# Storing the last column part of the last tile pair as two tiles on two queues

## Chip, cores, metric

One core of one Trainium2 chip. The metric is device time in microseconds (us), from repeated executions. The time before was 287.44 us, the median of 3 runs (287.15 to 287.49).

The span of a profile runs from the first to the last instruction of one execution; it is about 1.2 us shorter than the device time of that execution (286.2 and 287.46 us for the kernel before). I call "tail" the time from the end of the last evacuation out of PSUM to the end of the span. That is the part that the change can touch.

## The reference, cut to what matters

```python
# x is [1, 2048, 640], all bf16
g = sigmoid((x * gate_w).sum(-1, keepdims=True))
a = linear_attention(x, wqkv, w_phi) @ wo        # 32 heads of 20
b = (gelu(x @ w_gate) * (x @ w_up)) @ w_down     # hidden size 1728
return g * a + (1 - g) * b                       # [1, 2048, 640]
```

Only the final projections and the store of the output matter here. The kernel accumulates `@ wo` and `@ w_down` of a tile pair (2 x 128 rows) in PSUM, scales by a gate while it evacuates to SBUF, and stores.

## The kernel before

The work is laid out by hand, with explicit semaphores. A helper `sc.dma(queue, ...)` makes the issuing engine wait for everything the transfer reads, then issues; `sc.finish` makes SyncE wait for every engine and every DMA at the end. The last tile pair is done in three column parts (256, 256 and 128 columns), so that the first parts are stored while TensorE works on the next:

```python
def evac(h):                                   # column part h of the pair
    w0, w = sum(widths[:h]), widths[h]
    for j in (0, 1):                           # the two tiles of the pair
        bk, dst, g = banks[h][j], self.outsb[:, os_ + j, w0:w0 + w], self.Gm[:, ts[j]:ts[j] + 1]
        rd, wr = [("ps", bk), "Gm"], [("outsb", os_ + j, h)]
        if last and j == 1:
            sc.op("dve", lambda e: e.tensor_scalar(dst, self.bank(bk, w), g, None, op0=ALU.mult), reads=rd, writes=wr)
        else:
            sc.op("act", lambda e: e.activation(dst, self.bank(bk, w), AF.Copy, scale=g), reads=rd, writes=wr)
    if last:
        hs, c0, c1 = [h], w0, w0 + w
    # ... (other pairs: one store of all 640 columns; 'rows' is the output's view of the pair)
    sc.dma("sp", lambda e: e.dma_start(rows[:, :, c0:c1], self.outsb[:, os_:os_ + 2, c0:c1]),
           reads=[("outsb", os_ + j, k) for j in (0, 1) for k in hs], writes=[("out", t0, h)])
```

So tile 0 is evacuated by ScalarE and tile 1 by VectorE, and one store on SyncE's queue waits for both. The experiments also touch the warm-up, which keeps TensorE busy until the first load lands:

```python
for n in (512, 512, 512, 512, 512, 512, 128):
    sc.op("pe", lambda e: e.matmul(self.bank(0, n), ones[:, 0:P], ones[:, 0:n], start=True, stop=True),
          writes=[("ps", 0)])
```

The softmax here doesn't subtract the row's maximum and nothing guards it: scores larger than these inputs give would overflow.

Of the kernel before, what the change touches and what calls it, by code (L numbers as in the profile page):

```python
# [107 lines left out]
class _Kernel:  # L108
# [596 lines left out]
    def down_pair(self, t0, banks, widths):  # L705

        sc = self.sc
        ts = (t0, t0 + 1)
        NFC, KD = self.NFC - 1, self.KD
        nw = len(widths)  # L710
        hk = t0 // 4
        last = t0 + 2 == self.NT
        os_ = t0 % 4

        def mm(r, j, h, c, opens, x, n):
            t = ts[j]
            tt, gs, bk, w0, a = t % 4, t % 8, banks[h][j], sum(widths[:h]), 64 * r
            w, end = widths[h], x == n - 1
            if c <= NFC:
                lhs, rhs = self.hT(hk, c)[a:a + 64, tt * P:(tt + 1) * P], self.wd_sb[a:a + 64, c, w0:w0 + w]  # L720
                rd = [("hT", hk, c), "wd"] if c < NFC else [("hT", hk, 13, r), ("wd13", r)]
            else:
                k = c - NFC - 1
                lhs, rhs = self.goT[a:a + 64, gs, k, :], self.wo_sb[a:a + 64, k, w0:w0 + w]
                rd = [("goT", gs), "wo"]
            sc.op("pe", lambda e: e.matmul(self.bank(bk, w), lhs, rhs, start=opens and x == 0, stop=end and not opens,  # L726
                                           skip_group_check=True),
                  reads=rd, writes=[("ps", bk)] + ([("turn", bk)] if end else []), signal=end,
                  after=[("turn", bk)] if x == 0 and not opens else ())

        def evac(h):
            w0, w = sum(widths[:h]), widths[h]
            for j in (0, 1):
# [8 lines that stand above are left out]
            elif h == nw - 1:  # L742
                hs, c0, c1 = range(nw), 0, self.D
            else:
                return
            if t0 < self.TB:
                rows = self.out[0:self.BT, :].rearrange("(p j) n -> p j n", j=self.TB)[:, t0:t0 + 2, :]
            else:
                rows = self.out[t0 * P:(t0 + 2) * P, :].rearrange("(j p) n -> p j n", p=P)
            sc.dma("sp", lambda e: e.dma_start(rows[:, :, c0:c1], self.outsb[:, os_:os_ + 2, c0:c1]),  # L750
                   reads=[("outsb", os_ + j, k) for j in (0, 1) for k in hs], writes=[("out", t0, h)])

        wos = [NFC + 1 + k for k in range(KD)]
        opening = list(range(NFC + 1)) + wos
        for part in (range(NFC + 1), range(NFC + 1, len(opening))):
            for h in range(nw):
                for x in part:
                    for r in (0, 1):
                        mm(r, r, h, opening[x], True, x, len(opening))
                    yield None  # L760
        closing = list(range(NFC)) + wos
        for h in range(nw):
            for x, c in enumerate(closing):
                for r in (0, 1):
                    mm(r, 1 - r, h, c, False, x, len(closing))
                if c == closing[-1]:
                    evac(h)
                yield None
# [95 lines left out]
```

## Time and profile before

| What | Value |
|---|---|
| span | 286.2 us |
| TensorE busy | 281.8 us, 98% |
| last matmul starts | 283.49 us |
| last evacuation ends | 284.14 us |
| tail | 2.08 us |

The page of the kernel before, parts 1 and 4: busy time of each engine, and the chain of waits that ended last. TensorE is nearly the whole of both.

```profile
PE 281.8 (98%) x3017; PEld 186.7 (65%) x3032; DVE 174.9 (61%) x353; ACT 104.5 (37%) x199; POOL 5.3 (2%) x36
...
PE 98%; issue 0%; ACT 0%
```

The timeline of its end. Columns: start in us, length in us, engine, line, operation, tiles. SPq is SyncE's queue and ACTq ScalarE's; their length is that of the issue (the issuing engine's part in setting a transfer off), not of the transfer.

```profile
283.74 0.35 DVE L737 TENSOR_SCALAR outsb<-ps,Gm 128x128 bf16<-128x128 f32 x1 [0.52 <-PE ps L726]
283.77 0.37 ACT L739 ACTIVATE outsb<-ps,Gm 128x128 bf16<-128x128 f32 x1 [0.53 <-PE ps L726]
284.17 0.73 SPq L750 DMA_DIRECT2D out_dram<-outsb  x1
```

The issue begins right after both evacuations, and it is long: the stores of the first and of the second part took 0.370 and 0.372 us to issue, this one 0.735. It is not a wait for the data. The Trainium skill, "Perfetto Trace Analysis", section "Per-instruction lifecycle: what the profiler-reported window actually captures", says that the reported window of such a DMA opens when all its semaphores are satisfied, and that the movement of the data lies outside it. The trace agrees on both: the window opens at 284.17 with the evacuations done at 284.14, and the packets leave later, at 285.42. What fills the extra 0.36 us is then something behind the semaphores.

The DMA queues in the window from 283.5 to 284.6 us of the kernel before show one transfer on the instruction queue (q8); columns: packets, MB, share of 16 engines. The trace's single DMA records place it: one record of 16 KB at 283.56 to 284.52. I call it the fetch. It seems to sit on one DMA engine, as only one of the 16 completions of the store before came late (285.67, the others by 285.11).

```profile
q8 instruction: 1, 0.02, 5.4%
```

### The profile page before, as it was taken

The numbers are of one execution on the slowest core, as the hardware profiler recorded it, in microseconds if no ns is written. First come the engines' busy times: TensorE is split into PE (matmuls) and PEld (weight loads), VectorE is DVE, ScalarE is ACT, GpSimd is POOL, SyncE is SP. The second block draws the span as 40 slices with busy tenths as digits, with TensorE's granted clock in tenths as the row PEclk, the third lists the DMA queues.
The fourth block names the chain that finished last, engine by engine and source line by source line (L and its number), as shares of the span: only waits on it lengthen the run. The fifth ranks groups of instructions, "written<-read, shape, count | busy, mean of one in ns | idle before, by whom it ended". The sixth has DMA issues, their size and how long they took to land.

```text
span 286.2 us, 7006 instructions
## 1 busy us (share of the span) xinstructions
PE 281.8 (98%) x3017; PEld 186.7 (65%) x3032; DVE 174.9 (61%) x353; ACT 104.5 (37%) x199; POOL 5.3 (2%) x36
## 2 busy tenths in 40 slices
PE   8999999999999999999999999999999999999996
PEld 5566789999994444444444444445777777777785
DVE  2349999999976652567242334225883883883801
ACT  3367897678653222222323223221112112112111
POOL 7000000000000000000000000000000000000000
PEclk9999999999999999999999999999999999999999
DMA  8999996000002000011000000000232132222221
GB/s 226 206 176 236 367 366 201 0 2 2 2 0 48 0 0 0 3 24 23 2 0 0 0 2 0 0 0 2 25 84 62 45 48 81 61 49 72 70 72 48
DMA packets 36937, 18.67 MB, mean 65 GB/s; under 512 B 28970, under 2 KB 36394, under 8 KB 36906
## 3 DMA queue, kind: packets, MB, share of 16 engines
q1 hardware_dynamic: 36240, 18.19, 25.6%
q8 instruction: 24, 0.39, 0.6%
q10 hardware_dynamic: 666, 0.03, 0.2%
q14 instruction: 7, 0.06, 0.1%
HBM read 9.04 MB, written 2.62 MB: 41 GB/s over the span
## 4 chain that ended last, share of the span: by engine, by line
PE 98%; issue 0%; ACT 0%
PE ps L354 61%; PE ps L726 28%; PE ps L670 2%; PE ps L366 2%; PE ps L461 2%; PE ps L334 1%; PE ps L550 1%; PE ps L293 1%; ACT outsb L739 0%; PE ps L316 0%
## 5 line engine op out<-in xcount | busy, mean ns | idle before, releaser
L354 PE MATMUL ps<-xT,wg_sb 128*128 128x512 bf16 (+1 forms) x265 | 63.8, 379 | 0.4 <-issue 0.2
L354 PE MATMUL ps<-xT,wu_sb 128*128 128x512 bf16 (+1 forms) x263 | 63.3, 379 | 0.5 <-DVE hT L644 0.2
L642 ACT ACTIVATE gl<-ps 128x512 bf16<-128x512 f32 x52 | 30.9, 596 | 73.1 <-PE ps L354 68.7
L644 DVE TENSOR_TENSOR hT<-ps,gl 128x512 bf16<-128x512 f32 x39 | 26.7, 690 | 38.6 <-PE ps L354 38.5
L726 PE MATMUL ps<-wd_sb,hT 64*128 64x320 bf16 x648 | 48.5, 296 | 0.0
L354 PEld LDWEIGHTS ps<-xT,wu_sb 128*128 128x128 bf16 (+1 forms) x270 | 26.5, 99 | 29.8 <-DVE hT L644 0.5
L354 PEld LDWEIGHTS ps<-xT,wg_sb 128*128 128x128 bf16 (+1 forms) x270 | 26.2, 99 | 29.0 <-ACT gl L642 0.2
L354 PE MATMUL ps<-w,xT 128*64 128x512 bf16 (+6 forms) x398 | 41.5, 325 | 0.1
L739 ACT ACTIVATE outsb<-ps,Gm 128x320 bf16<-128x320 f32 (+2 forms) x31 | 14.5, 515 | 72.4 <-PE ps L726 72.4
L726 PEld LDWEIGHTS ps<-wd_sb,hT 64*128 64x128 bf16 x648 | 31.1, 94 | 12.2 <-issue 0.4
L354 PEld LDWEIGHTS ps<-w,xT 128*64 128x64 bf16 (+1 forms) x400 | 35.9, 107 | 4.5
L726 PE MATMUL ps<-wo_sb,goT 64*128 64x320 bf16 (+2 forms) x340 | 26.5, 288 | 0.0
L354 PE MATMUL ps<-xT,wq 128*64 128x512 bf16 (+1 forms) x184 | 26.0, 380 | 0.1
L431 DVE TENSOR_REDUCE Dk<-Ek 128x64 f32<-128x1280 bf16 x16 | 23.7, 1479 | 3.6 <-ACT gcol L419 3.6
L445 DVE TENSOR_TENSOR Ek<-Ek,Dk 128x640 bf16<-128x640 bf16 x32 | 25.0, 821 | 0.6
L697 DVE TENSOR_TENSOR O<-ps,RH 128x640 bf16<-128x640 f32 x32 | 24.8, 816 | 0.0
L416 ACT ACTIVATE Ek<-ps 128x640 bf16<-128x640 f32 x32 | 20.7, 703 | 4.2 <-PE ps L354 4.2
L530 ACT ACTIVATE Eq<-ps 128x512 bf16<-128x512 f32 x40 | 21.6, 607 | 0.6 <-PE ps L354 0.4
L644 DVE TENSOR_TENSOR xT<-ps,gl 128x512 bf16<-128x512 f32 x13 | 9.0, 691 | 18.2 <-PE ps L354 18.2
L726 PEld LDWEIGHTS ps<-wo_sb,goT 64*128 64x128 bf16 x340 | 16.0, 94 | 5.3
L354 PEld LDWEIGHTS ps<-xT,wq 128*64 128x64 bf16 (+1 forms) x185 | 15.4, 108 | 2.9
L726 PE MATMUL ps<-wd_sb,xT 64*128 64x320 bf16 (+2 forms) x270 | 16.0, 269 | 0.0
(69 smaller groups left out, 174.8 us busy)
## 6 DMA issues: line engine op xcount, KB each, us to landing
out_dram<-outsb SPq DMA_DIRECT2D x7, 320.0 KB, 2.3
wd_sb<-in_B_w_down_dram SPq DMA_DIRECT2D x1, 2080.0 KB, 13.9
wg_sb<-in_B_w_gate_dram SPq DMA_DIRECT2D x1, 1120.0 KB, 6.2
wu_sb<-in_B_w_up_dram SPq DMA_DIRECT2D x1, 1120.0 KB, 9.8
wg_sb<-in_B_w_gate_dram SPq DMA_DIRECT2D x1, 960.0 KB, 9.8
wu_sb<-in_B_w_up_dram SPq DMA_DIRECT2D x1, 960.0 KB, 10.2
w<-in_A_wqkv_dram SPq DMA_DIRECT2D x5, 160.0 KB, 4.0
wo_sb<-in_A_wo_dram SPq DMA_DIRECT2D x1, 800.0 KB, 9.2
```

The lines of the kernel that those rows point to most:

```text
L354: self.sc.op("pe", lambda e: e.matmul(self.ps[a:z, bank * 512 + c0:bank * 512 + c0 + n], lhs[:, a:z], rhs, start=first, stop=fin), reads=r ...
L366: sc.op("pe", lambda e, c0=c0, n=n, bk=bk, col=col: e.matmul(self.bank(bk)[:, col:col + n], self.xT[:, kt, t * P:(t + 1) * P], self.w3[:, ...
L416: self.sc.op("act", lambda e, s=s, scale=scale: e.activation(self.Ek[:, se, s, :], self.ps[:, o:o + self.D], AF.Exp, scale=scale), reads=[ ...
L431: sc.op("dve", lambda e: e.tensor_reduce(self.Dk[:, se, 0, :].rearrange("p (s h) -> p s h", h=H), self.Ek[:, se, :, :].rearrange("p s (h d ...
L445: sc.op("dve", lambda e, v=v, r=r: e.tensor_tensor(v, v, r, ALU.mult), reads=[("Rk", se)], writes=[("Ek", se, s)])
L461: sc.op("pe", lambda e: e.matmul(self.ps[a:a + 64, b * 512 + c:b * 512 + c + 2 * nf], va[:, lo:lo + 64], self.Ek[:, se, :, f0:f0 + nf], st ...
L530: sc.op("act", lambda e, s=s, scale=scale: e.activation(self.Eq[:, s, i, b * self.BT:(b + 1) * self.BT], self.bank(bank), AF.Exp, scale=sc ...
L642: sc.op("act", lambda e: e.activation(self.gl[:, slot, :], self.bank(banks[0]), AF.Gelu_apprx_tanh), reads=[("ps", banks[0])], writes=[("g ...
L644: sc.op("dve", lambda e: e.tensor_tensor(hT, self.bank(banks[1]), self.gl[:, slot, :], ALU.mult), reads=[("ps", banks[1]), ("gl", slot)], ...
L697: dve(lambda e, o=o, f=f, s=s: e.tensor_tensor(o, V[s][:, :, :, 0:DH], f, ALU.mult), rb + [key(6 + s)], [("O", s, sl)], guard=old)
L726: sc.op("pe", lambda e: e.matmul(self.bank(bk, w), lhs, rhs, start=opens and x == 0, stop=end and not opens, skip_group_check=True), reads ...
L739: sc.op("act", lambda e: e.activation(dst, self.bank(bk, w), AF.Copy, scale=g), reads=rd, writes=wr)
```

## The change

The intent: let tile 1's store leave as soon as VectorE is done and tile 0's as soon as ScalarE is done, each on a queue of its own.

```diff
+            if last and h == nw - 1:
+                for j, q in ((0, "act"), (1, "sp")):
+                    sc.dma(q, lambda e: e.dma_start(rows[:, j, c0:c1], self.outsb[:, os_ + j, c0:c1]),
+                           reads=[("outsb", os_ + j, h)], writes=[("out", t0 + j, h)])
+                return
             sc.dma("sp", lambda e: e.dma_start(rows[:, :, c0:c1], self.outsb[:, os_:os_ + 2, c0:c1]),
                    reads=[("outsb", os_ + j, k) for j in (0, 1) for k in hs], writes=[("out", t0, h)])
```

The diff has no other line. A few matmul records are missing in the trace of the kernel before (3017 against 3032).

## The prediction

> **What bounds the kernel.** The page: TensorE is busy 281.8 of 286.2 us, and the chain of waits is 98% TensorE. The change touches no matmul: both kernels list the same TensorE and VectorE instructions; ScalarE gains one store, SyncE's last store halves. Only the tail after the last matmul can move. Timeline and DMA records (us from the span's start):
>
> - the last matmuls signal at 283.72 and 283.75;
> - VectorE evacuates tile 1 (0.35 us; done 284.10), ScalarE tile 0 (0.37 us; done 284.15);
> - the SyncE store waits for both and issues 284.17 to 284.90: 0.735 us, where the two stores before took 0.37 each;
> - its packets run 285.42 to 285.82 (256 rows of 256 bytes), completions land 285.98 to 286.18, the span ends at 286.22.
>
> The tail from the end of evacuation is 2.07 us, 0.7% of the time. No repair of it can give 2%.
>
> **What the change does.**
> 1. Tile 1's store need not wait for ScalarE: it may issue at 284.12 instead of 284.17. Tile 0's store still waits for ScalarE's evacuation and starts on ScalarE's queue at about 284.17. The later store decides, so this alone gives about 0.
> 2. Each store has half the rows. In this trace the issue hardly depends on that (0.36 us for 128 rows, 0.37 for 256), nor does issue to first packet (0.86 and 0.89): about 0.02 us saved. The bytes are the same, so the 0.40 us of packets is not halved if both are in flight together. The Trainium skill, "DMA: Bandwidth & Descriptors", section "Issuing engines are not separate DMA queues", says so: stores from different engines interleave on the same 16 DMA engines, and only issue time is saved. This trace has no two concurrent stores to test it.
> 3. What might give: the last issue is 0.36 us longer than its like. It seems held by an instruction fetch (16 KB, 283.56 to 284.52) on one DMA engine, which also delayed the store before (last completion 285.67, the others by 285.11); the issue ends 0.38 us after that fetch. Two transposes overtaken by such fetches were stretched alike (1.74 and 2.12 us instead of 1.20). If the hold belongs to SyncE's queue, ScalarE's store escapes it, and SyncE's, with half the packets, ends about 0.2 us earlier. If it holds every issue, nothing is gained. I think the second a little likelier.
> 4. Added: one DMA and one semaphore for the final wait. The final waits cost 0.06 us each but run at 284.95 to 285.41, before the landing; at most 0.06 shows.
>
> Early in the run ScalarE and SyncE issued loads concurrently at 0.43 us each, so a collision of issues should cost at most 0.1 us.
>
> **Sum.** Gain 0 to 0.25 us, loss up to 0.1. Predicted 287.36 us (before 287.44), range 286.95 to 287.70, mostly the scatter of runs (287.15 to 287.49). Faster by over 2%: 0.005; within 2%: 0.99; slower: 0.005.
>
> **What would show it.** Last matmul and evacuations at the same times (within 0.2 us). In the timeline of the end: issues at about 284.12 (SyncE) and 284.17 (ScalarE), packets between 285.0 and 285.8, the span ending 1.8 to 2.1 us after the last evacuation. Step 3 is right if SyncE's issue stays near 0.7 us, ScalarE's is near 0.4 and the fetch is in the same place.
>
> **What would make it wrong.** A first store on ScalarE's queue after 280 us of quiet may start slower than one on SyncE's; the issues may serialise (0.3 us slower); or the fetch falls elsewhere, moving the tail by 0.4 us. None reaches 2%.

## The result, and the profile after

The changed kernel took 287.77 us (median of 6 runs, 287.55 to 288.01) beside 287.47 us (6 runs, 287.15 to 288.72) of the kernel before. The ratio is 1.0, with a 95% interval of 0.9979 to 1.0021: the same. A ratio here is the mean time of one kernel's fast runs over the mean of the other's fast runs of the same rounds, so it is not quite the ratio of the medians. Timed again in five rounds on one chip, the two medians were both 287.44 us and the ratio 1.0001 (0.9986 to 1.0016).

The timeline of the end of the changed kernel, columns as above:

```profile
283.97 0.35 DVE L737 TENSOR_SCALAR outsb<-ps,Gm 128x128 bf16<-128x128 f32 x1 [0.52 <-PE ps L726]
284.00 0.37 ACT L739 ACTIVATE outsb<-ps,Gm 128x128 bf16<-128x128 f32 x1 [0.53 <-PE ps L726]
284.35 0.82 SPq L752 DMA_DIRECT2D out_dram<-outsb  x1
284.40 0.37 ACTq L752 DMA_DIRECT2D out_dram<-outsb  x1
```

Two stores start 0.05 us apart. SyncE's issue is long again; ScalarE's has the normal length. The DMA queues from 283.7 to 284.8 us of the changed kernel show the fetch again, at 283.76 to 284.76 in the DMA records:

```profile
q8 instruction: 1, 0.02, 5.7%
```

The tail went from 2.08 to 2.00 us, a gain of 0.08 us, or 0.03% of the time. Yet the profiled span grew from 286.22 to 286.37 us, because everything before the tail was 0.23 us later. That is not the change's doing. The matmuls of line 726, the projections, show it. First those of the kernel before (the columns are the least, median and greatest length in ns, and the first and last start in us):

```profile
L726 PE MATMUL ps<-wd_sb,hT x648: 296/296/307, 197.5 to 261.8; 64*128 64x320 bf16 x162
L726 PE MATMUL ps<-wo_sb,goT x340: 216/296/298, 201.7 to 283.5; 64*128 64x320 bf16 x140, 64*128 64x256 bf16 x20, 64*128 64x128 bf16 x10
```

The same two lines of the changed kernel:

```profile
L726 PE MATMUL ps<-wd_sb,hT x648: 296/296/307, 197.8 to 262.0; 64*128 64x320 bf16 x162
L726 PE MATMUL ps<-wo_sb,goT x340: 216/296/298, 202.0 to 283.7; 64*128 64x320 bf16 x140, 64*128 64x256 bf16 x20, 64*128 64x128 bf16 x10
```

The first projection starts at 197.54 us before and 197.77 after, the last at 283.49 and 283.72: 85.95 us between them in both. The 0.23 us was there long before the changed lines ran. Over all eleven profiled executions the first of these matmuls starts anywhere from 196.96 to 198.74 us, and the distance to the last stays at 85.95 (85.946 to 85.948). Already at the first matmul that folds the query weights (line 334), 21 us into the run, the starts are spread as widely (20.90 to 22.68). So the scatter of these executions before the tail arises in the first 21 us, while the kernel loads its inputs (why was not tested), and the effect of a change at the end has to be read from the tail.

### The profile page after: what moved, and what is told of

Its sections match the earlier page's. It is cut to its first block, busy times and chain, and to the rows that moved or that the text cites. A ratio compares the mean times of both kernels' runs of the same rounds, so it can differ in the third digit from the quotient of the medians.

```text
span 286.4 us, 7022 instructions
## 1 busy us (share of the span) xinstructions
PE 283.0 (99%) x3032; PEld 186.8 (65%) x3032; DVE 174.9 (61%) x353; ACT 104.6 (37%) x199; POOL 5.3 (2%) x36
## 3 DMA queue, kind: packets, MB, share of 16 engines
HBM read 9.04 MB, written 2.62 MB: 41 GB/s over the span
## 4 chain that ended last, share of the span: by engine, by line
PE 98%; DMA 1%; ACT 0%; issue 0%
PE ps L354 62%; PE ps L726 28%; PE ps L670 2%; PE ps L366 2%; PE ps L461 2%; PE ps L334 1%; DMA xtok<-in_A_x_dram 1%; PE ps L293 1%; ACT outsb L739 0%; PE ps L316 0%
## 5 line engine op out<-in xcount | busy, mean ns | idle before, releaser
L354 PE MATMUL ps<-xT,wg_sb 128*128 128x512 bf16 (+1 forms) x270 | 64.9, 379 | 0.0
L354 PE MATMUL ps<-xT,wu_sb 128*128 128x512 bf16 (+1 forms) x270 | 64.8, 379 | 0.0
```

Source lines behind the costliest of these rows:

```text
L354: self.sc.op("pe", lambda e: e.matmul(self.ps[a:z, bank * 512 + c0:bank * 512 + c0 + n], lhs[:, a:z], rhs, start=first, stop=fin), reads=r ...
```

## The experiments

Three theories for the long last issue:

- **Theory 1.** An instruction fetch occupies one DMA engine; a queue that still has an earlier store to get out to that engine cannot issue its next until the fetch ends. SyncE's queue has the middle part's store, issued 0.8 to 0.9 us before; ScalarE's has none.
- **Theory 2.** The distance alone: a queue holds any store that follows another by under 0.9 us.
- **Theory 3.** Any issue from SyncE during a fetch is held.

All numbers, in us from the traces. "Fetch end" is the end of the last 16 KB instruction fetch in the DMA records. Two entries are two profiled executions.

| Kernel | SyncE's last issue | ScalarE's last issue | fetch end | end of the last held issue minus fetch end | tail |
|---|---|---|---|---|---|
| before | 0.735 | none | 284.52 | 0.38 | 2.08 |
| after | 0.822; 0.974 | 0.366; 0.370 | 284.76; 284.28 | 0.40; 0.39 | 2.00; 2.14 |
| swap_c2 | 0.345 | 0.621 | 284.35 | 0.39 | 1.94 |
| one_queue | 1.000, then 0.383 | none | 284.15 | 0.38 (first store) | 2.62 |
| merged_act | none | 0.407 | 284.39 | not held | 1.91 |
| shift_before | 0.372; 0.373 | none | 282.01; 283.20 | not held | 1.72; 1.72 |
| shift_after | 0.344 | 0.368 | 282.41 | not held | 1.76 |
| shift_half | 0.372 | none | 284.18 | not held | 1.72 |
| big_pending | 0.442 | none | 284.67 | 0.39 | 2.33 |

All nine runs gave the reference's result.

**swap_c2: the earlier store on the other queue.** The changed kernel, with the middle part's store on ScalarE.

```diff
-            sc.dma("sp", lambda e: e.dma_start(rows[:, :, c0:c1], self.outsb[:, os_:os_ + 2, c0:c1]),
+            sc.dma("act" if last and h == 1 else "sp", lambda e: e.dma_start(rows[:, :, c0:c1], self.outsb[:, os_:os_ + 2, c0:c1]),
```

> The changed kernel, with the store of the middle column part (issued 0.8 us before the last ones) moved to ScalarE's queue. Theory 1 (ring): the hold is on the queue that still has that earlier store pending on the DMA engine busy with the instruction fetch. Then it changes sides: ScalarE's last issue is 0.7 to 0.85 us, SyncE's falls from 0.82 to about 0.37. Theory 2 (spacing): a queue holds any store that follows another by under 0.9 us, fetch or no fetch: the same picture. Theory 3 (SyncE): any SyncE issue during the fetch is held: SyncE's stays 0.8, ScalarE's 0.37. Tail from the end of the last evacuation to the end of the span: 1.9 to 2.1 us (changed kernel 1.99) under all three, total within 0.3%.

Measured: the hold changed sides. The timeline of the end of swap_c2:

```profile
284.07 0.34 SPq L752 DMA_DIRECT2D out_dram<-outsb  x1
284.12 0.62 ACTq L752 DMA_DIRECT2D out_dram<-outsb  x1
```

SyncE's issue began during the fetch (283.42 to 284.35) and had the normal length, so theory 3 falls. ScalarE's 0.62 us is below the 0.7 to 0.85 that I wrote down, because the fetch ended sooner after the issue began; the issue ended 0.39 us after it. Device time 287.18 us (4 runs), ratio 0.9981 (0.9959 to 1.0003).

**one_queue: the split alone.** Both halves on SyncE's queue, VectorE's tile first.

```diff
-                for j, q in ((0, "act"), (1, "sp")):
+                for j, q in ((1, "sp"), (0, "sp")):
```

> The split alone: two tiles, both on SyncE's queue, VectorE's tile first. All theories: the first issue held to about 0.8 us, the second (about 0.37 us) only after it, its packets following about 0.3 to 0.5 us later. Tail 2.2 to 2.5 us, longer than before's 2.07 and the changed kernel's 1.99: so the split alone loses 0.1 to 0.4 us. Total within 0.3%.

Measured: the first issue took 1.00 us (I had expected about 0.8), the second, begun only after it, 0.38 us; tail 2.62 us, above the range that I gave (2.2 to 2.5), as the fetch ended 0.59 us after the evacuation here and 0.38 us after it in before. Device time 288.21 us (4 runs), ratio 1.0017 (0.9991 to 1.0042). Counted from the end of the fetch, which the held store waits for, the span ends 2.03 us later here and 1.70 us later in before: the split on one queue costs 0.33 us in these two traces.

**merged_act: the queue alone.** The kernel before, with only the last store, unsplit, on ScalarE's queue.

```diff
-            sc.dma("sp", lambda e: e.dma_start(rows[:, :, c0:c1], self.outsb[:, os_:os_ + 2, c0:c1]),
+            sc.dma("act" if last and h == nw - 1 else "sp", lambda e: e.dma_start(rows[:, :, c0:c1], self.outsb[:, os_:os_ + 2, c0:c1]),
```

> The queue alone: the kernel before with its last, unsplit store on ScalarE's queue. Theories 1, 2 and 3 agree: issue 0.37 us (not 0.735), first packet about 0.88 us after it, tail 1.7 us if the engine that the fetch delayed has caught up by then, 1.9 us if its backlog still holds the last completion. If instead halving the rows is what helps, the tail stays at 2.0 to 2.1.

Measured: issue 0.407 us, inside the fetch (283.23 to 284.39) and not held by it; first packet 0.93 us after the issue began; tail 1.91 us. Moving the store to the idle queue gains 0.17 us against before's tail, more than the change as made did with its split and its two queues (one trace each; the fetch ended 0.50 us after the evacuation here and 0.38 us after it in before, so the place of the fetch did not favour it). The tail is not the 1.72 us of a run without the fetch: a store is reported as landed by 16 completions; the fifteenth of this store's landed at 285.62 us and the last at 285.76, and in the kernels whose fetch came early (shift_before) those two are 0.013 us apart. Of the middle store's 256 packets, 240 were done by 284.50, and the other 16 went out one after the other from the end of the fetch until 285.10. I read this as the backlog of the engine that fetched, the second case that I had written down. Device time 287.11 us (4 runs), ratio 0.9983 (0.9961 to 1.0005).

**shift_before: the fetch moved.** Each trace has 24 fetches of 16 KB on q8. If they bring TensorE's instructions block by block, more of these at the start move the last fetch forward at the end. The warm-up's columns stay the same, and it took the same 2.83 us.

```diff
-        for n in (512, 512, 512, 512, 512, 512, 128):
+        for n in [64] * 50:
```

> The kernel before with its warm-up as 50 matmuls of 64 columns in place of 7 of up to 512 (the same 3200 columns): 86 more TensorE instructions at the start, so that the last instruction fetch comes about 2 us earlier at the end. Theories 1 and 3 (the fetch holds the store): last issue 0.37 us, tail 1.65 to 1.75 us instead of 2.07. Theory 2 (spacing): issue stays 0.73 us, tail 2.07. The whole may be up to 1.5 us longer if the warm-up takes longer; the tail is what is compared.

Measured, the DMA queues from 281.1 to 282.1 us of shift_before:

```profile
q8 instruction: 1, 0.02, 5.5%
```

And the timeline of its end:

```profile
283.48 0.35 DVE L737 TENSOR_SCALAR outsb<-ps,Gm 128x128 bf16<-128x128 f32 x1 [0.52 <-PE ps L726]
283.51 0.37 ACT L739 ACTIVATE outsb<-ps,Gm 128x128 bf16<-128x128 f32 x1 [0.53 <-PE ps L726]
283.91 0.37 SPq L750 DMA_DIRECT2D out_dram<-outsb  x1
```

The fetch now lies at 281.13 to 282.01, the last issue takes 0.37 us, and the tail is 1.72 us. The store still follows the middle one by 0.87 us, so theory 2 falls. The difference in the tail, 0.36 us, is the length of the hold (0.735 less 0.372). Device time 286.85 us (4 runs), ratio 0.9973 (0.9955 to 0.999): more than the tail can give.

**after_again and shift_before_again: both timed in five rounds, beside the kernel before on one chip.**

```diff
 no edit: the changed kernel and shift_before as they were
```

> The change, timed again beside the kernel before on one chip. Theory 1 (a queue with a pending store on the engine that fetches is held until the fetch ends): SyncE's issue ends about 0.39 us after the fetch, ScalarE's takes 0.37; tail 1.95 to 2.05 us. Ratio to before 0.999 to 1.001: the tail's 0.08 us is 0.03%.

> Theory 1: as in its first run the fetch comes 2 us before the end of the matmuls, the last issue takes 0.37 us, the tail 1.70 to 1.75 us. Ratio to before 0.9975 to 0.9995: the tail gives 0.35 us (0.12%); what is beyond that is scatter of the front.

Measured: after_again 287.44 us (6 runs), ratio 1.0001 (0.9986 to 1.0016). Its tail was 2.14 us, above the 1.95 to 2.05 that I expected, because this time the fetch ended 0.56 us after the evacuation (in the first profile 0.40 us); the rule held, with the issue ending 0.39 us after the fetch. shift_before_again: tail 1.72 us as in its first run, issue 0.373; 287.17 us (6 runs), ratio 0.9994 (0.9981 to 1.0008). Its profiled execution had a longer span than any other (287.06 us), most of it from the loading phase: its first matmul with the query weights came at 22.68 us, 1.2 us later than before's (21.47). So the gain of the tail is steady in the traces, and the device time does not resolve it.

**shift_after: the change without the fetch.**

```diff
 (the changed kernel)
-        for n in (512, 512, 512, 512, 512, 512, 128):
+        for n in [64] * 50:
```

> The change, with the fetch out of the way. Theory 1: both issues 0.37 us, SyncE's from about 0.03 us before ScalarE's evacuation ends; what the split is worth without the hold is at most the 0.02 us of issue and part of the 0.40 us of packets: tail 1.60 to 1.75 us (1.72 for the unsplit store so shifted). If it is 1.5 or less, the split itself was worth something that the fetch hid; if over 1.8, two queues cost something by themselves.

Measured, the timeline of its end:

```profile
284.31 0.34 SPq L752 DMA_DIRECT2D out_dram<-outsb  x1
284.36 0.37 ACTq L752 DMA_DIRECT2D out_dram<-outsb  x1
```

Neither is held. The tail is 1.76 us, 0.04 us longer than shift_before's 1.72 (a little above the 1.75 that I gave as the upper end). The packets of the two halves leave at 285.15 to 285.44 and 285.27 to 285.56: together 0.41 us, where the unsplit store takes 0.40. This agrees with the Trainium skill, "DMA: Bandwidth & Descriptors", section "Issuing engines are not separate DMA queues", which says that the DMAs of two issuing engines interleave on the same 16 DMA engines. The two end waits came one after the other, at 286.01 and 286.07 us, with the last completion at 285.99; in shift_before there is one, at 285.58, after a landing at 285.56. Without the hold the split gains nothing and costs one wait. Device time 287.81 us (5 runs), ratio 1.0011 (0.9998 to 1.0024).

**shift_half: a smaller shift.** 36 more TensorE instructions instead of 86.

```diff
-        for n in (512, 512, 512, 512, 512, 512, 128):
+        for n in [128] * 25:
```

> The kernel before with the warm-up as 25 matmuls of 128 columns: 36 more instructions in place of 86, so that the fetch comes about 0.5 to 0.9 us earlier than in before and overlaps the second store's issue at 283.3 us. Theory 1: if the fetch begins while the first store's packets (about 282.3 to 282.8) are still to be sent, the second store's issue is held and ends 0.39 us after the fetch; if it begins after them, the second takes 0.37. The last store's issue is 0.37 us if the fetch is over before it starts or before the second's packets start; tail then 1.7 us. Theory 2 (spacing, 0.87 us between the last two stores): last issue 0.73, tail 2.07.

Measured: the fetch lay at 283.19 to 284.18, the middle store was issued inside it at 283.57 and not held (0.372), the last at 284.44 after it (0.372), tail 1.72 us. The last issue, begun after the fetch, so tells against theory 2 only; theory 1 is tested by the middle one. One data packet of the first part's store was still to be sent, and left only at 284.16. So theory 1 as I had worded it (any store pending on the fetching engine) is too wide: one leftover packet did not hold the next issue. Device time 287.52 us (4 runs), ratio 0.9999 (0.9982 to 1.0015).

**big_pending: what exactly holds.** Theory 1 leaves two readings: how many rows are pending (1a), or whether the earlier store was being handed over to the engines when the fetch was on (1b). This kernel writes the previous pair's rows a second time, with the same values, so that many rows are pending whose packets started before the fetch.

```diff
 (shift_half)
+            if last and h == 0:
+                old = self.out[(t0 - 2) * P:t0 * P, :].rearrange("(j p) n -> p j n", p=P)
+                sc.dma("sp", lambda e: e.dma_start(old, self.outsb[:, os_ - 2:os_, :]),
+                       reads=[("outsb", os_ - 2 + j, k) for j in (0, 1) for k in (0, 1)], writes=[("out", t0 - 2, 1)])
```

> What exactly holds an issue. The half-shifted kernel (25 warm-up matmuls; its fetch came 0.6 us earlier, and the issue that followed a nearly drained store was not held), plus one extra store right behind the first part's: the rows of the pair before, written a second time (same values), 256 rows of 1280 bytes, so that its packets run from about 1 us before the second store's issue until after it. The fetch should begin after the first packets of the extra store have left and end after the second store's issue begins. Theory 1a (how much is pending): a queue with over some 20 rows pending on the engine that fetches is held: here about 12 of the extra store and 17 of the second; the second store's issue ends 0.39 us after the fetch. Theory 1b (handing over): only a store whose packets had not yet started when the fetch began holds the next issue: the second store's issue takes 0.37 us, and the last store's is held only if it starts before the fetch ends. Tail 1.7 us if the last is not held.

Measured: the extra store's packets began at 283.21, the fetch lay at 283.42 to 284.67, and the middle store's issue at 283.71, inside the fetch, took 0.373 us. Part of the extra store was plainly waiting: 16 of its 256 rows left only after the fetch, the last at 285.8, and its last completion landed at 286.33, the other fifteen by 284.60. Reading 1a, which asked for a hold here, falls. The last store's issue, begun 0.05 us before the fetch ended, took 0.442 us and so ended 0.39 us after it, as 1b asks. Timed once each: 288.13 us beside 288.78 of before.

The timeline of SyncE's last two issues:

```profile
283.70 0.37 SPq L750 DMA_DIRECT2D out_dram<-outsb  x1
284.61 0.44 SPq L750 DMA_DIRECT2D out_dram<-outsb  x1
```

What stands for these stores: an issue is held to the end of the fetch when the store ahead of it on the same queue was handed over while the fetch was on. Handed over means here that its packets began. The packets of the last pair's stores that found their queue free began 0.84 to 0.94 us after their issue began, and in before that moment of the middle store (284.18) lies inside the fetch. That it is the handing over that blocks is inferred from these times; no record shows it directly. One rival is left untested: in all six held issues the store ahead had been issued only 0.82 to 0.91 us before, and no run has a later issue during the same fetch. A rule of spacing and fetch together (any issue within about 0.9 us of the one ahead, if a fetch is on) would fit as well.

The same traces show the hold on a wider scale, and there it needs no store close ahead. Of the 176 transposes of line 702 (SyncE's queue, 16 in each of the eleven traces), 37 took 1.30 to 2.68 us. Every one of these met a fetch and ended 0.35 to 0.45 us after it, and no issue had begun on the queue in the 3 us before. The other 139 took at most 1.21 us; 18 of them met a fetch too, one that ended within 0.72 us of the transpose's start or began 0.78 us or more after it. So for a transpose it matters whether a fetch is on about 0.8 us after its start, and what is said above of the store ahead is not the whole rule.

## Why the prediction was right or wrong

- **"Only the tail after the last matmul can move"; no 2%.** Right. The projections take 85.95 us before and after; the tail gained 0.08 us.
- **Step 1, SyncE's issue at 284.12 and ScalarE's at 284.17.** Right once the shift of the whole run (0.23 us) is taken off: 284.35 and 284.40. It gave nothing: SyncE's issue was held in after, and in shift_after, where it was not, the tail was no shorter.
- **Step 2, half the rows save about 0.02 us and the packets are not halved.** Right: issues of 0.344 us on SyncE's queue against 0.372 unsplit, and of 0.368 on ScalarE's against 0.407 (merged_act); and 0.41 us of packets for both halves together in shift_after.
- **Step 3, the long issue is held by an instruction fetch.** Right: moving the fetch took the hold away. "If the hold belongs to SyncE's queue, ScalarE's store escapes it": this happened. The step that failed is "I think the second a little likelier", that every issue is held; ScalarE's issue of 0.366 us, during SyncE's of 0.822, settles it. The term "ends about 0.2 us earlier" was mis-sized: counted from the end of the fetch, the span ends 1.70 us later in before and 1.60 and 1.58 us later in the two runs of after, a gain of 0.10 to 0.12. SyncE's half has 0.27 us of packets in place of 0.40. In the tail only 0.08 us of it showed in the first run, and nothing in the second (2.14 us), since the fetch fell differently against the evacuation. That the first run's 0.08 us equals the gain in the predicted total (287.44 to 287.36) is luck: it stood for a gain between 0 and 0.25, as I did not know whether ScalarE's queue would be held too.
- **Step 4, the final wait.** Right: its price was hidden under the hold in after, and about 0.06 us of it shows in shift_after.
- **"A first store on ScalarE's queue after 280 us of quiet may start slower"; "the issues may serialise".** Neither happened: its first packet came 0.87 us after the issue, and the two issues overlapped.
- **The number.** 287.36 us was predicted. The first median, 287.77, lies just above my range (286.95 to 287.70), the second, 287.44, inside it, and the ratio to before is 1.0 in both. The range was drawn from three runs of before (287.15 to 287.49), which was too narrow: the six of the comparison covered 287.15 to 288.72. In the profiled executions the scatter arises in the loading phase, which I had not looked at.

A version that beats both by its tail is shift_before, a change of one line in the warm-up: 1.72 us against 2.08 and 2.00. In device time it is ahead in both comparisons, clear of noise only in the first.

## What to carry to other kernels

When the last transfer of a kernel looks slow, first compare its issue with that of its like, and look for what else its DMA engines carry at that moment; the store that was held behind its own queue gained from an idle queue or from moving the disturbance, and not from being split. Moving it is no lasting repair: here 36 more TensorE instructions brought the last fetch about 0.6 us forward against the projections and 86 more 2.2 to 2.5 us, so any later edit of TensorE's instructions may bring it back. Two queues share the engines: two halves together took as long as the whole. And when a change touches a microsecond at the end of a run whose beginning scatters by more, read the tail in several traces instead of the total.

## What the Trainium skill lacked or had wrong

- "DMA: Bandwidth & Descriptors" (section "Issuing engines are not separate DMA queues") says that several issuing engines only save the time that issuing takes. The bandwidth part held (0.41 against 0.40 us of packets). It lacks that a queue can be held on its own while the other is free: 0.82 us for SyncE's issue, 0.37 for ScalarE's at the same time; and 0.35 and 0.62 the other way round when the earlier store changed queues.
- No page says that the fetch of TensorE's instructions (16 KB; the last one took 0.9 to 1.25 us on one engine here) delays stores: a hold of 0.36 us in before, ending 0.38 to 0.40 us after the fetch in all six held issues, and a last completion of the middle store that landed 0.56 us after its other fifteen in before and 0.65 in after. The 37 long transposes point the same way (1.30 to 2.68 us beside 1.21 at most).
- "Perfetto Trace Analysis" (section "Per-instruction lifecycle: what the profiler-reported window actually captures") fills the reported window of such a DMA with a wait for the exclusive lock of the descriptor generator, the generation itself and the semaphore update. It names no wait of the queue's own. In before no other engine issued a transfer near the end, and the window was still 0.36 us longer than its like; and in after ScalarE's issue of 0.366 us ran wholly inside SyncE's of 0.822, so the held SyncE did not keep it out. The runs do not show in which part of the window SyncE waited, so the page is not shown to be wrong.
